# Linear attention with a gated FFN: loads of batch 2 no longer held for a weight, another buffer for batch 3's keys, an earlier wait for the weight load, a sketch by transposes, and a rebuilt order

## The chip, the cores and the metric

The kernel runs on one core of a Trainium2 chip. The metric is the device time of one execution in microseconds (us); lower is better. A profile also has a span, from the first to the last instruction of the profiled execution; it is some 2 us shorter than the time (97.4 against 95.4 in the profiled run of before). Runs are sorted by state: one over 1.5% above the fastest of its kernel counts as slow, and ratios use fast runs only. The engines are TensorE (PE in the views; PEld is its weight loads), VectorE (DVE), ScalarE (ACT), GpSimd (POOL) and SyncE (SP), which here issues loads and stores; a q behind a name means its sequencer.

## The reference

```python
# attention: batch 4, heads 4, seq 1088, head_dim 32, r = 8
phi(x) = outer(S1 x, S2 x).reshape(r * r)         # a polynomial sketch, 64 features
kv  = einsum('bhsf,bhsd->bhfd', phi(k), v);  z = sum_s phi(k)
out = einsum('bhsf,bhfd->bhsd', phi(q), kv) / (einsum(phi(q), z) + 1e-6)
# FFN on x = out, heads side by side (d_model 128, d_ff 1024)
x_prev = x shifted by one token
xk, xr = mu * x + (1 - mu) * x_prev               # with mu_k and mu_r
k = relu(xk @ w_k);  v = (k * k) @ w_v
result = sigmoid(xr @ w_r) * v
```

A batch's keys must all be summed into its state (kv, z) before its queries give x, and x opens its FFN.

## The kernel before

Each task has a name, an engine and a place in one long list; each engine does its tasks in the list's order. Those that matter here: KTb (DVE transposes the keys of batch b), KP and KA (projection, accumulation), QTb (DVE transposes the queries), Q1g (projection of the g-th of ten query groups), XK (the FFN's input, on DVE), M1 (first FFN product), Z (products of zeros that keep TensorE's clock up), DL3k, DL3v, DL3q (loads of batch 3). The other names in the cuts can be passed over.

```python
ORDER = """
SS/PE/b0 SM/DVE SC3/ACT SC1/POOL SC2/ACT SF/ACT KT0_0/DVE Z/4 S4T/PE/b0 S4E/ACT KT0_1/DVE Z/2 KP0_0/PE/b0 KE0_0/DVE
... (cut)
QX1/PE/b3 KT2_0/DVE KB1/ACT Q13/PE/b0 KT2_1/DVE XL0/ACT XP0/ACT XF0/POOL XB0/ACT KP2_0/PE/b1 QN2/DVE XP1/ACT DL3k/DMA
XK0/DVE QF2_1/POOL RR0/PE/b4 QE3/ACT XB1/ACT XK1/DVE M10_5/PE/b2 M10_3/PE/b5 SG0/ACT DL3v/DMA M10_2/PE/b6 KE2_0/ACT
... (cut)
"""
# input buffers: three sets for four batches
hdk.append(hdk[2]); hdq.append(hdq[1]); vt.append(vt[1])      # batch 3 shares
# SyncE's queue, in order: k0 v0 q0 k1 wr v1 q1; then, in the task WL,
def load_w():
    nc.gpsimd.tensor_copy(wk[:, :1], hdq[0][:, 0, :1])        # makes the weights wait for q0
    nc.gpsimd.dma_start(wk[:], moe_w_k)
    nc.gpsimd.dma_start(wv[:] ...)
    nc.sync.dma_start(turn[:], wk[:1, :1])                    # the "turn": SyncE waits for wk
    load_k(2, nc.sync); load_v(2, nc.sync); load_q(2, nc.sync)
add("DL3k", ..., load_k(3, nc.sync), ["KT2_0", "KT2_1"])      # k3 goes where k2 was
add("DL3v", ..., load_v(3, nc.sync), ["DL3k", "KA1_0_0", "KA1_1_0"])
add("DL3q", ..., load_q(3, nc.sync), ["DL3v", "QT1_0", "QT1_1"])
# the sketch: two products with an identity
nc.tensor.matmul(p[:, x * R:x * R + R], S8[:, x]..., ident[:R, :R], skip_group_check=True)
```

## Time and profile before

| | before |
|---|---|
| time, median (lowest to highest) | 97.13 us (96.3 to 97.21) |
| profiled span | 95.4 us |
| busy: PE, DVE, ACT, POOL | 81.9, 73.1, 64.4, 53.9 us |
| first FFN product; last product | 26.53; 88.11 us |

The prediction shows the busy slices, the chain of waits, the queue's waits and the stretches. One more view: busy time in two stretches, up to 40 us and from there on. Columns: stretch, length, then PE, PE's weight loads, DVE, ACT and POOL busy with instruction counts, granted clock, DMA share, GB/s.

```profile
0.00:40.00 40.00, 33.90 (x595) 24.62 (x595) 26.71 (x79) 19.49 (x62) 17.45 (x38) 1.00 0.70 184
40.00:96.00 56.00, 48.01 (x668) 35.38 (x668) 46.34 (x103) 44.95 (x84) 36.41 (x35) 0.96 0.18 42
```

DVE did 26.71 us of its work in the first 40 and left 46.34 us for the rest, during which it has hardly a hole.

### The profile page before, as it was taken

The page shows a single profiled execution, that of the slowest core. Times are in us where ns is not written, and L with a number is a line of the kernel's source. Part 1 is how long each engine was busy: PE and PEld are TensorE (multiplying, and loading weights), DVE is VectorE, ACT ScalarE, POOL GpSimd, SP SyncE. Part 2 cuts the span into 40 slices and gives each one's busy share as a digit, 9 for nine tenths or more (in the row PEclk, how much of TensorE's full clock was granted, in tenths as well). Part 3 has the DMA queues.
Part 4 walks back from the last instruction along what each step waited for, and adds up shares of the span by engine and source line. Part 5 has one row for each costly group of instructions (what it writes and reads, how often), then busy time and mean ns, then how long its engine had stood idle before and what let it go on. Part 6 is the DMA issues. An engine that isn't in the chain of part 4 may idle for free.

```text
span 95.4 us, 3142 instructions
## 1 busy us (share of the span) xinstructions
PE 81.9 (86%) x1263; PEld 60.0 (63%) x1263; DVE 73.1 (77%) x181; ACT 64.4 (68%) x146; POOL 53.9 (56%) x72
## 2 busy tenths in 40 slices
PE   5999989699589866899999999999999999999000
...
DVE  4062998983795449999998998999899999997200
ACT  0630144146399699199999979668999999999000
...
DMA  2899999248978910011000021051400000532620
...
DMA packets 8668, 9.71 MB, mean 102 GB/s; under 512 B 716, under 2 KB 7502, under 8 KB 8654
## 3 DMA queue, kind: packets, MB, share of 16 engines
...
q0 software_dynamic: 416, 0.52, 3.2%
...
q8 instruction: 10, 0.16, 0.7%
q14 instruction: 4, 0.03, 0.1%
...
## 4 chain that ended last, share of the span: by engine, by line
PE 40%; ACT 21%; DMA 15%; DVE 9%; issue 5%; POOL 2%; SPq 1%; ACTq 1%; DVEq 0%
ACT k L628 9%; PE ps_h L620 8%; DMA hdq<-in_q_dram 7%; ACT k L639 6%; PE ps_o L649 6%; DMA hdk<-in_k_dram 5%; PE ps_qtp L555 4%; PE wt L262 4%; PE ps_abw L510 4%; DMA S<-in_S_dram 3%; PE ps_kv L417 3%; PE ps_kab L386 3%; PE ps_x L576 2%; ACT r L667 2%; DVE kT L379 2%
## 5 line engine op out<-in xcount | busy, mean ns | idle before, releaser
L637 POOL TENSOR_TENSOR k<-k 128x1024 bf16<-128x1024 bf16 (+2 forms) x18 | 28.4, 1588 | 5.9 <-ACT k L628 3.6
L628 ACT ACTIVATE k<-ps_h 128x512 bf16<-128x512 f32 (+3 forms) x48 | 23.0, 541 | 1.4 <-PE ps_h L620 1.2
L620 PE MATMUL ps_h<-XK,wk 128*128 128x512 bf16 (+3 forms) x80 | 20.1, 350 | 0.4 <-DVE XK L589 0.3
L630 DVE TENSOR_SCALAR k<-ps_h 128x512 bf16<-128x512 f32 (+3 forms) x32 | 19.4, 639 | 0.6 <-PE ps_h L620 0.4
L639 ACT ACTIVATE k<-k 128x1024 bf16<-128x1024 bf16 (+3 forms) x19 | 18.5, 1010 | 1.6 <-DVE k L630 1.5
L649 PE MATMUL ps_o<-wv,k 128*128 128x128 bf16 x272 | 18.6, 219 | 0.1
L649 PEld LDWEIGHTS <-k 128*128 128x128 bf16 x272 | 16.2, 98 | 3.5 <-ACT k L639 0.9
L369 POOL TENSOR_TENSOR kp<-ab 128x512 f32<-128x512 f32 (+1 forms) x7 | 8.8, 1261 | 9.9 <-DVE ab L276 6.1
L369 POOL TENSOR_TENSOR qp<-an,wsb 128x512 f32<-128x512 f32 x8 | 8.5, 1072 | 6.2 <-PE ps_qtp L555 3.4
L620 PEld LDWEIGHTS <-wk 128*128 128x128 bf16 x80 | 7.6, 116 | 4.6 <-issue 1.9
L555 PE MATMUL ps_qtp<-ident,qp 128*128 128x128 f32 x68 | 9.7, 278 | 0.5 <-DVE qp L369 0.5
L386 PE MATMUL ps_kab<-SW,kT 128*64 128x64 f32 x144 | 7.0, 246 | 2.7 <-DVE kT L379 2.7
L386 PEld LDWEIGHTS ps_kab<-SW,kT 128*64 128x64 f32 x144 | 5.9, 156 | 4.9 <-ACT XB L274 2.4
L510 PE MATMUL ps_abw<-SW,qT 128*64 128x96 f32 (+1 forms) x120 | 8.3, 258 | 0.4 <-ACT SW L274 0.3
L555 PEld LDWEIGHTS ps_qtp<-ident,qp 128*128 128x128 f32 x68 | 7.5, 142 | 1.7 <-DVE qp L369 0.6
L379 DVE STREAM_TRANSPOSE kT<-hdk 128x256 f32<-128x256 f32 (+1 forms) x16 | 6.0, 428 | 3.0 <-DMA hdk<-in_k_dram 3.0
L510 PEld LDWEIGHTS ps_abw<-SW,qT 128*64 128x64 f32 (+1 forms) x120 | 6.5, 144 | 2.6 <-ACT kvS L274 1.0
L262 PE MATMUL wt<-zero 128*128 128x512 f32 (+2 forms) x10 | 6.8, 795 | 1.0 <-DVE one L161 1.0
L493 DVE STREAM_TRANSPOSE qT<-hdq 128x832 f32<-128x832 f32 (+1 forms) x8 | 5.6, 703 | 2.6 <-DMA hdq<-in_q_dram 2.6
L274 ACT COPY qpT<-ps_qtp 128x512 f32<-128x512 f32 (+1 forms) x13 | 6.6, 543 | 0.7 <-PE ps_qtp L555 0.6
L417 PE MATMUL ps_kv<-kp,vt 128*32 128x64 f32 x288 | 6.2, 223 | 0.9 <-issue 0.9
L667 ACT ACTIVATE r<-ps_r 128x512 f32<-128x512 f32 (+3 forms) x10 | 5.5, 550 | 2.1 <-PE ps_r L662 2.0
...
## 6 DMA issues: line engine op xcount, KB each, us to landing
...
```

Of the source, the lines that this page charges most:

```text
L262: nc.tensor.matmul(wt[:, :m * P], zero[:], _ap(zero[:], [[0, m], [1, P]]), skip_group_check=True)
L369: eng.tensor_mul(o.rearrange("p t h i j -> p (t h) i j"), _ap(a_, [[sa, y], [1, R], [0, R]]), _ap(b_, [[sb, y], [0, R], [1, R]]))
L386: nc.tensor.matmul(p[64 * c:64 * c + 64, (t - t0) * 64:(t - t0) * 64 + 64], kT[b][:, t, 64 * c:64 * c + 64], SW[:, 0, :H, :2, :], skip_gro ...
L417: nc.tensor.matmul(kv[32 * h:32 * h + 32, :64], vt[b][:, h, T, :], kp[:, t, h].rearrange("p i j -> p (i j)"), start=(T == 0), stop=(T == 8 ...
L510: nc.tensor.matmul(p[lo:hi, t * 96:t * 96 + 96], qT[:, s + lo:s + hi], SW[:, (s + lo) // S, g % 2:g % 2 + H].rearrange("p h x r -> p (h x ...
L555: nc.tensor.transpose(p[:, t * P:t * P + P], qp[g][:, t, 2 * pair:2 * pair + 2].rearrange("p h i j -> p (h i j)"), ident[:])
L620: nc.tensor.matmul(h[:, :n * P], wkc[:, c // 4, c % 4], XK[:, F0[g] * P:(F0[g] + n) * P])
L628: nc.scalar.activation(o, i, RELU)
L630: nc.vector.tensor_scalar(o, i, 0.0, None, op0=mybir.AluOpType.max)
L637: (nc.vector if eng == "DVE" else nc.gpsimd).tensor_mul(k2[:, :, :n * P], k1[:, :, :n * P], k1[:, :, :n * P])
L639: nc.scalar.activation(k2[:, :, :n * P], k1[:, :, :n * P], mybir.ActivationFunctionType.Square)
L649: nc.tensor.matmul(o[:, t * P:t * P + P], k2s[g, j][:, c, t * P:t * P + P], wv[:, w * j + c, :], start=(j == 0 and c == 0 and t == 0), sto ...
```

## The change

The intent: no hole in the queue of loads, batch 3's keys loaded earlier, a shorter front, and a list of tasks rebuilt around that.

```diff
-    hdk.append(hdk[2])
-    hdq.append(hdq[1])
-    vt.append(vt[1])
+    for x in (hdk, hdq, vt):
+        x.append(x[1])
...
     load_q(1, nc.sync)
+    load_k(2, nc.sync)
+    load_v(2, nc.sync)
+    load_q(2, nc.sync)
     def load_w():
-        nc.gpsimd.tensor_copy(wk[:, :1], hdq[0][:, 0, :1])
+        nc.gpsimd.tensor_copy(wk[:, :1], vt[0][:, 0, 0, :1])
         ... (wk and wv as before)
-        nc.sync.dma_start(turn[:], wk[:1, :1])
-        load_k(2, nc.sync)
-        load_v(2, nc.sync)
-        load_q(2, nc.sync)
-    add("WL", {"POOL": 1.6}, lambda e: load_w(), ["Lq0"])
+    add("WL", {"POOL": 1.6}, lambda e: load_w(), ["Lv0"])
-    add("DL3k", ..., ["KT2_0", "KT2_1"])
+    add("DL3k", ..., ["KT1_0", "KT1_1"])
-    nc.tensor.matmul(p[:, x * R:x * R + R], S8[:, x]..., ident[:R, :R], skip_group_check=True)
+    nc.tensor.transpose(p[:, x * R:x * R + R], S8[:, x]..., ident[:R, :R])
-    wsb: bufs=2      K2B: {2: 8, 4: 1}
+    wsb: bufs=3      K2B: {2: 7, 4: 1}
 ORDER (cut: the whole list is new, with other engines for some tasks)
-... SF/ACT KT0_0/DVE Z/4 S4T/PE/b0 ... Z/2 KP0_0 ... Z/4 KA0_0_0
+... SF/ACT SC2/POOL Z/2 S4T/PE/b0 KT0_0/DVE ... Z/2 KP0_0 ... Z/5 KA0_0_0
-... KT2_0 KB1 Q13 KT2_1 ... XK0 ... XK1 M10_5 ...
+... XK0 KG1 XK1 KW1 M10_1 M10_3 M10_0 KT2_1 ... KT2_0 ...
```

More of the change, by code (lines that the diff above doesn't have):

```diff
@@ L28 @@
 ORDER = """
-SS/PE/b0 SM/DVE SC3/ACT SC1/POOL SC2/ACT SF/ACT KT0_0/DVE Z/4 S4T/PE/b0 S4E/ACT KT0_1/DVE Z/2 KP0_0/PE/b0 KE0_0/DVE
-KP0_1/PE/b1 KF0_0_1/DVE KF0_0_0/POOL KE0_1/ACT KF0_1_0/DVE Z/4 KA0_0_0/PE/b0 KA0_0_1/PE KF0_1_1/DVE KA0_1_0/PE
-QT0_1/DVE WL/POOL KA0_1_1/PE MU/PE/b1 KC0/ACT KZ0/DVE QT0_0/DVE OM/ACT KD0/PE/b0 KG0/PE KW0/ACT KT1_0/DVE Q10/PE/b1
-KB0/ACT WRP/ACT KT1_1/DVE WRC/ACT KP1_0/PE/b0 Q11/PE/b2 QE0/DVE KE1_0/ACT QP0/DVE KP1_1/PE/b3 QD0/DVE KF1_0_1/POOL
-KF1_0_0/DVE QE1/ACT QI0/DVE KE1_1/ACT QP1/DVE QN0/DVE QD1/DVE KF1_1_1/DVE KF1_1_0/POOL KA1_0_0/PE/b0 QI1/DVE QF0_0/DVE
@@ L34 @@
-Q12/PE/b7 QN1/DVE QF1_0/DVE QR0_0/PE/b1 KA1_1_0/PE QE2/ACT QT1_0/DVE QV0_0/ACT QP2/DVE QT1_1/DVE QR1_0/PE/b2 KC1/ACT
-QR0_1/PE/b1 QR1_1/PE/b3 QV0_1/ACT KZ1/DVE QV1_1/ACT QD2/DVE KD1/PE/b0 QV1_0/DVE KG1/PE QI2/DVE KW1/DVE QY0/PE/b2
-QX1/PE/b3 KT2_0/DVE KB1/ACT Q13/PE/b0 KT2_1/DVE XL0/ACT XP0/ACT XF0/POOL XB0/ACT KP2_0/PE/b1 QN2/DVE XP1/ACT DL3k/DMA
-XK0/DVE QF2_1/POOL RR0/PE/b4 QE3/ACT XB1/ACT XK1/DVE M10_5/PE/b2 M10_3/PE/b5 SG0/ACT DL3v/DMA M10_2/PE/b6 KE2_0/ACT
-QP3/DVE RR1/PE/b3 RE0_2/DVE RE0_5/ACT M11_5/PE/b4 QF2_0/POOL QD3/DVE RE0_3/ACT M11_2/PE/b6 KF2_0_0/DVE SG1/ACT
@@ L39 @@
-M11_6/PE/b2 Q14/PE/b5 RE1_2/ACT DL3q/DMA RE1_5/ACT QI3/DVE KF2_0_1/DVE RE1_6/ACT M11_0/PE/b6 SQ0_1/POOL M11_3/PE/b3
-M10_4/PE/b4 QE4/ACT QR2_1/PE/b7 QN3/DVE RE0_4/ACT KT3_0/DVE RE1_0/ACT QR2_0/PE/b1 QF3_1/POOL RE1_3/ACT M11_7/PE/b6
-QV2_1/ACT M11_1/PE/b4 QF3_0/DVE M10_1/PE/b3 KP2_1/PE/b2 RE1_7/ACT RE0_1/DVE SQ1_1/POOL QV2_0/ACT M10_0/PE/b7 RE1_1/DVE
-M10_6/PE/b6 QR3_1/PE/b0 RE0_6/ACT QT3_1/DVE SQ1_0/ACT QR3_0/PE/b1 SQ1_3/POOL KA2_0_0/PE/b6 QV3_1/ACT QT3_0/DVE
-QV3_0/ACT M21_0/PE/b4 KT3_1/DVE M21_1/PE RE0_0/ACT M11_4/PE/b0 SQ0_2/ACT M10_7/PE/b1 QY2/PE/b3 SQ0_0/POOL QX3/PE/b7
@@ L44 @@
-KE2_1/ACT QT2_0/DVE RE0_7/ACT QP4/DVE RE1_4/ACT KF2_1_0/POOL KF2_1_1/DVE SQ1_2/ACT KP3_1/PE/b0 QD4/DVE XB2/ACT
-QT2_1/DVE M21_2/PE M20_0/PE/b1 XP2/ACT M20_1/PE M21_3/PE SQ0_3/POOL M20_2/PE KE3_1/DVE KA2_1_0/PE XL1/ACT XB3/ACT
-XK2/DVE XF1/POOL XP3/ACT M20_3/PE RR2/PE/b2 KF3_1_1/POOL KZ2/DVE FN1/DVE RR3/PE/b3 KC2/ACT FN0/DVE SG2/ACT OD1_0/DMA
-XK3/DVE M12_5/PE/b6 M12_4/PE/b1 XE0/POOL SG3/ACT OD1_1/DMA KD2/PE/b4 KF3_1_0/POOL QI4/DVE KG2/PE RE2_5/ACT OD0_0/DMA
-RE2_4/DVE M13_0/PE/b3 KW2/ACT M13_2/PE/b7 KB2/ACT QN4/DVE M13_5/PE/b6 SQ2_2/ACT RE3_0/DVE Q15/PE/b4 QF4_1/DVE
@@ L49 @@
-QF4_0/POOL M13_3/PE/b3 RE3_2/ACT M13_1/PE/b0 QE5/DVE Q16/PE/b1 RE3_3/ACT RE3_1/DVE RE3_5/ACT M13_4/PE/b7 SQ3_1/POOL
-QP5/DVE QR4_0/PE/b3 QE6/DVE SQ3_0/ACT QD5/DVE M13_7/PE/b6 QP6/DVE M13_6/PE/b0 QI5/DVE QR4_1/PE/b5 QV4_0/DVE RE3_7/ACT
-M23_0/PE/b2 RE3_4/ACT QN5/DVE QV4_1/DVE M12_6/PE/b3 RE3_6/ACT M12_7/PE/b6 QF5_1/POOL M12_3/PE/b7 QF5_0/DVE M23_1/PE
-SQ3_2/ACT KP3_0/PE/b5 QY4/PE/b0 RE2_7/DVE SQ3_3/POOL QR5_1/PE/b4 RE2_3/ACT RE2_6/DVE QR5_0/PE/b6 KE3_0/ACT QD6/DVE
-QV5_1/ACT M23_2/PE KF3_0_0/DVE QV5_0/ACT M12_0/PE/b3 QI6/DVE M12_2/PE/b4 M12_1/PE/b7 QN6/DVE RE2_0/ACT KF3_0_1/POOL
@@ L54 @@
-QX5/PE/b6 RE2_2/DVE RE2_1/ACT QF6_1/DVE SQ2_0/ACT SQ2_1/POOL M23_3/PE QF6_0/DVE KA3_0_0/PE/b5 FN3/DVE XL2/ACT XP4/ACT
-QR6_1/PE/b1 XP5/DVE XB4/ACT OD3_3/DMA KA3_1_0/PE QV6_1/ACT OD3_4/DMA XK4/DVE XF2/POOL RR4/PE/b2 XB5/ACT OD3_1/DMA
-XE1/POOL QR6_0/PE/b1 KZ3/DVE KC3/DVE OD3_2/DMA SG4/ACT XK5/DVE SQ2_3/POOL M14_0/PE/b5 OD3_0/DMA M14_1/PE/b0 QV6_0/ACT
-M14_5/PE/b7 RE4_0/DVE M14_3/PE/b2 KD3/PE/b6 RE4_3/ACT M14_2/PE/b1 RE4_1/DVE M14_4/PE/b5 KG3/PE RE4_2/ACT RE4_5/DVE
-M14_7/PE/b0 RE4_4/ACT M14_6/PE/b2 SQ4_1/POOL QY6/PE/b1 M15_7/PE/b4 RE4_7/DVE KW3/ACT M22_0/PE/b7 RE4_6/ACT RE5_7/DVE
@@ L59 @@
-Q17/PE/b5 KB3/ACT M22_1/PE QE7/DVE M22_2/PE QP7/DVE SQ4_2/POOL M22_3/PE QD7/DVE SQ4_0/ACT QI7/DVE Q19/PE/b4 QN7/DVE
-M15_3/PE/b6 FN2/DVE M15_2/PE/b2 SQ4_3/ACT M15_6/PE/b0 QF7_1/DVE M24_0/PE/b3 OD2_1/DMA M24_1/PE QF7_0/POOL RE5_2/DVE
-OD2_2/DMA RE5_3/ACT M24_2/PE OD2_3/DMA QE9/DVE SQ5_1/ACT M24_3/PE RE5_6/DVE OD2_0/DMA Q18/PE/b2 QP9/DVE FN4/DVE
-SQ5_3/ACT QR7_0/PE/b0 QD9/DVE QE8/DVE OD4_0/DMA QR7_1/PE/b3 QI9/DVE QV7_0/ACT QP8/DVE OD4_1/DMA RR5/PE/b5 QN9/DVE
-QD8/DVE QV7_1/ACT QF9_0/POOL OD4_2/DMA M15_0/PE/b0 QI8/DVE M15_5/PE/b6 QN8/DVE SG5/ACT OD4_3/DMA M15_4/PE/b7 QF8_0/DVE
@@ L64 @@
-QX7/PE/b3 RE5_0/ACT QF8_1/POOL RE5_4/DVE RE5_5/ACT QR9_1/PE/b0 QR9_0/PE/b7 XL3/DVE XP6/ACT SQ5_2/POOL XP7/DVE
-M15_1/PE/b6 QR8_1/PE/b2 XB6/ACT XK6/DVE QR8_0/PE/b4 XB7/ACT RR6/PE/b5 QV9_1/DVE RE5_1/ACT M16_0/PE/b1 QV8_0/DVE
-M16_4/PE/b0 SG6/ACT M16_6/PE/b6 XE2/POOL QV9_0/DVE RE6_4/ACT M16_1/PE/b4 XF3/POOL QV8_1/DVE M16_7/PE/b5 RE6_0/ACT
-SQ5_0/POOL RR7/PE/b0 RE6_1/DVE RE6_7/ACT M16_5/PE/b1 XK7/DVE RE6_6/ACT M16_3/PE/b2 M16_2/PE/b5 QY8/PE/b4 QX9/PE/b7
-SG7/ACT RE6_3/DVE SQ6_3/ACT SQ6_0/POOL RE6_5/DVE M17_1/PE/b2 M17_3/PE/b0 RE6_2/ACT XP8/DVE M17_2/PE/b3 M25_0/PE/b1
@@ L69 @@
-SQ6_2/ACT RE7_3/DVE M17_6/PE/b5 M25_1/PE RE7_6/DVE RE7_2/ACT M17_5/PE/b0 SQ6_1/POOL M17_7/PE/b6 XK8/DVE RE7_1/ACT
-M25_2/PE M26_0/PE/b3 RE7_5/ACT RE7_7/DVE M18_4/PE/b2 XB8/ACT M18_7/PE/b5 XP9/DVE M18_5/PE/b0 RE8_4/ACT M17_0/PE/b6
-RE8_7/DVE M18_3/PE/b4 SQ7_3/ACT XE3/POOL M25_3/PE RE8_3/DVE M26_1/PE SQ7_1/POOL FN5/DVE RE7_0/ACT M26_2/PE RE8_5/ACT
-M26_3/PE XK9/DVE OD5_1/DMA SQ7_0/ACT RR8/PE/b1 FN6/DVE OD5_2/DMA M18_1/PE/b0 M17_4/PE/b6 OD5_0/DMA M18_0/PE/b4
-RE8_1/ACT SQ8_2/POOL M18_2/PE/b3 RE7_4/DVE OD6_0/DMA M27_0/PE/b5 SG8/ACT OD6_1/DMA RE8_0/DVE M27_1/PE SQ7_2/ACT
@@ L74 @@
-OD6_3/DMA M18_6/PE/b1 RE8_2/DVE M19_1/PE/b6 OD6_2/DMA M19_5/PE/b4 M19_3/PE/b0 SQ8_0/ACT RE8_6/DVE M27_2/PE OD5_3/DMA
-M27_3/PE RE9_5/DVE SQ8_3/POOL SQ8_1/ACT M19_2/PE/b1 RE9_3/DVE M28_0/PE/b3 FN7/DVE M19_6/PE/b4 M19_0/PE/b0 RE9_1/ACT
-M28_1/PE RE9_6/DVE RE9_2/ACT OD7_2/DMA M28_2/PE RE9_0/ACT SQ9_1/DVE OD7_4/DMA M19_4/PE/b4 XB9/ACT M19_7/PE/b1
-SQ9_0/DVE OD7_1/DMA M28_3/PE RE9_4/ACT RE9_7/ACT OD7_3/DMA RR9/PE/b7 SQ9_2/DVE M29_0/PE/b4 OD7_0/DMA SQ9_3/ACT FN8/DVE
-M29_1/PE M29_2/PE SG9/ACT OD8_3/DMA M29_3/PE OD8_2/ACT OD8_1/DMA FN9/DVE OD8_0/ACT OD9_2/ACT OD9_0/ACT OD9_1/ACT
+SS/PE/b0 SM/DVE SC3/ACT SC1/POOL SF/ACT SC2/POOL Z/2 S4T/PE/b0 KT0_0/DVE S4E/ACT KT0_1/DVE Z/2 KP0_0/PE/b0 KE0_0/ACT
@@ new lines @@
+KP0_1/PE/b1 KF0_0_1/POOL KF0_0_0/DVE KE0_1/ACT KF0_1_0/DVE KF0_1_1/POOL Z/5 KA0_0_0/PE/b0 KA0_0_1/PE WL/POOL
+KA0_1_0/PE QT0_1/DVE KA0_1_1/PE MU/PE/b1 KC0/ACT KZ0/DVE QT0_0/DVE OM/ACT KD0/PE/b0 KG0/PE KW0/ACT KT1_0/DVE Q11/PE/b1
+WRP/POOL Q10/PE/b2 KB0/DVE KT1_1/DVE QE1/ACT WRC/POOL KP1_0/PE/b0 QE0/ACT QP1/DVE Q12/PE/b3 QP0/DVE QD1/DVE KE1_0/ACT
+QD0/DVE QI1/DVE QI0/DVE QN1/DVE KF1_0_0/POOL QN0/DVE QF1_0/DVE KP1_1/PE/b7 QE2/ACT KF1_0_1/DVE QR1_1/PE/b1 DL3k/DMA
+QF0_0/POOL KE1_1/ACT QR1_0/PE/b4 QP2/DVE KA1_0_0/PE/b0 QV1_1/DVE QV1_0/ACT KF1_1_1/DVE KF1_1_0/POOL QR0_0/PE/b2
@@ new lines @@
+QD2/DVE QR0_1/PE/b4 QI2/DVE QV0_0/DVE QV0_1/ACT QT1_0/DVE QY0/PE/b4 QX1/PE/b2 QT1_1/DVE KA1_1_0/PE XL0/ACT XP0/ACT
+XB0/DVE XF0/POOL XP1/ACT QN2/DVE KZ1/DVE DL3v/DMA KC1/ACT QF2_0/POOL XB1/ACT KD1/PE/b7 XK0/DVE KG1/PE XK1/DVE KW1/ACT
+M10_1/PE/b4 M10_3/PE/b0 M10_0/PE/b1 KT2_1/DVE Q13/PE/b5 KB1/ACT QF2_1/POOL RE0_1/ACT DL3q/DMA RE0_3/ACT RE0_0/ACT
+M11_2/PE/b4 KT2_0/DVE M11_4/PE/b0 M11_5/PE/b1 QE3/ACT M11_7/PE/b7 M11_6/PE/b2 RE1_4/ACT M11_0/PE/b6 SQ0_0/POOL QP3/DVE
+RE1_5/ACT M11_3/PE/b3 RE1_2/DVE M10_4/PE/b0 RE1_0/ACT KP2_0/PE/b1 SQ1_2/POOL QD3/DVE RE1_6/ACT RE1_3/DVE RE0_4/ACT
@@ new lines @@
+RE1_7/ACT M20_0/PE/b6 QI3/DVE M10_5/PE/b2 M10_2/PE/b4 M10_7/PE/b0 SQ1_1/ACT QR2_1/PE/b3 QN3/DVE RE0_2/DVE QF3_0/DVE
+QR2_0/PE/b7 RE0_7/ACT SQ0_1/POOL RE0_5/ACT QV2_1/ACT M11_1/PE/b0 QF3_1/DVE RR1/PE/b2 M10_6/PE/b4 RE1_1/ACT M20_1/PE
+SG1/ACT RR0/PE/b3 QT2_1/DVE KP2_1/PE/b0 SQ1_0/POOL SQ1_3/ACT RE0_6/ACT QR3_0/PE/b2 KE2_0/ACT QT2_0/DVE QV2_0/ACT
+QR3_1/PE/b4 SQ0_3/POOL KE2_1/DVE SQ0_2/ACT Q14/PE/b5 QV3_0/DVE KF2_0_1/POOL QV3_1/ACT KF2_1_1/DVE QY2/PE/b7 M20_2/PE
+SG0/ACT M20_3/PE QX3/PE/b4 FN0/DVE KF2_0_0/POOL KT3_0/DVE OD0_0/DMA M21_0/PE/b6 QE4/DVE M21_1/PE XP2/ACT XB3/DVE
@@ new lines @@
+KF2_1_0/POOL M21_2/PE KA2_0_0/PE/b1 XB2/ACT XK2/DVE M21_3/PE RR2/PE/b3 XP3/DVE M12_0/PE/b7 M12_1/PE/b2 SG2/ACT
+KA2_1_0/PE FN1/DVE XE0/POOL RE2_0/ACT KT3_1/DVE OD1_0/DMA M12_4/PE/b6 RE2_1/ACT M12_5/PE/b3 OD1_1/DMA M12_2/PE/b7
+KC2/DVE RE2_4/ACT KZ2/DVE M12_6/PE/b0 RE2_5/DVE KD2/PE/b1 SQ2_0/ACT KG2/PE RE2_6/DVE SQ2_2/POOL M12_7/PE/b3
+M12_3/PE/b6 KB2/DVE KP3_1/PE/b2 KW2/ACT QT3_1/DVE RE2_2/ACT Q15/PE/b1 RE2_3/ACT QP4/DVE RE2_7/ACT XL1/DVE Q16/PE/b6
+QT3_0/DVE SQ2_1/ACT XF1/POOL QD4/DVE M22_0/PE/b3 QI4/DVE QN4/DVE KP3_0/PE/b7 SQ2_3/ACT XK3/DVE QF4_0/POOL M22_1/PE
@@ new lines @@
+KE3_0/DVE M22_2/PE QE5/ACT QF4_1/DVE QE6/ACT KF3_0_1/POOL M22_3/PE KE3_1/ACT QP5/DVE M13_1/PE/b4 KF3_0_0/DVE
+M13_2/PE/b5 QR4_0/PE/b0 RE3_1/ACT KF3_1_0/POOL QD5/DVE FN2/DVE KA3_0_0/PE/b7 RE3_2/ACT QV4_0/ACT QI5/DVE M13_4/PE/b4
+OD2_3/DMA KF3_1_1/DVE M13_0/PE/b5 QR4_1/PE/b3 OD2_1/DMA RE3_0/ACT QN5/DVE M13_3/PE/b0 QP6/DVE OD2_2/DMA QF5_0/POOL
+QF5_1/DVE KA3_1_0/PE RE3_3/ACT OD2_0/DMA QV4_1/DVE M13_5/PE/b5 SQ3_1/ACT M13_7/PE/b0 SQ3_0/POOL M13_6/PE/b2 QD6/DVE
+QR5_0/PE/b3 KZ3/DVE RE3_4/DVE QR5_1/PE/b1 KC3/ACT RE3_6/ACT QI6/DVE KD3/PE/b7 QY4/PE/b4 QN6/DVE QV5_0/ACT KG3/PE
@@ new lines @@
+QV5_1/DVE KW3/ACT RR3/PE/b2 RE3_5/ACT KB3/DVE QF6_1/POOL QF6_0/DVE QX5/PE/b1 RE3_7/ACT SQ3_2/ACT SQ3_3/POOL Q17/PE/b0
+XP4/DVE XL2/ACT XB4/ACT QR6_1/PE/b6 XB5/DVE QE7/ACT RR4/PE/b5 SG3/ACT QP7/DVE Q18/PE/b7 XP5/ACT XK4/DVE XF2/POOL
+M23_0/PE/b2 QD7/DVE SG4/ACT QV6_1/DVE XE1/POOL M14_7/PE/b4 M14_1/PE/b3 QI7/DVE M14_5/PE/b5 RE4_7/DVE M14_4/PE/b6
+RE4_1/ACT M23_1/PE QN7/DVE RE4_4/ACT M14_0/PE/b4 RE4_5/DVE QF7_1/POOL M14_3/PE/b3 M23_2/PE RE4_0/ACT QF7_0/DVE
+M14_2/PE/b5 SQ4_2/ACT M14_6/PE/b6 RE4_3/DVE SQ4_0/POOL QR6_0/PE/b4 QR7_0/PE/b0 QE8/DVE RE4_2/ACT QV6_0/DVE QR7_1/PE/b3
```

37 lines of the change are left out of this document (28 added, 9 removed).

## The prediction

> **What bounds the kernel now.** I read four views of the trace before the change: the busy slices, the chain that ended last, the queue's own waits, and busy time by stretch. In the slices (40 of 2.385 us each; tenths busy):
>
> ```profile
> PE   5999989699589866899999999999999999999000
> DVE  4062998983795449999998998999899999997200
> ACT  0630144146399699199999979668999999999000
> DMA  2899999248978910011000021051400000532620
> ```
>
> Two regimes show. From slice 17 (about 40 us) to slice 36 all three compute engines stand at 8 to 9 tenths; before that they have holes, and the DMA row falls to 2 and 4 tenths in slices 7 and 8 (16.7 to 21.5 us) though seven of the twelve q, k, v loads are still to come. The chain names the hole; its columns are start, length, what:
>
> ```profile
> 18.71 0.56 SPq L233
> 19.27 0.05 issue
> 19.32 5.11 DMA hdk<-in_k_dram
> 24.43 0.03 issue
> 24.45 0.07 DVE kT L379
> ...
> 28.30 6.27 DMA hdq<-in_q_dram
> 34.57 0.02 issue
> 34.59 0.05 DVE qT L493
> ```
>
> L233 is the "turn": a one-element copy that makes SyncE hold the loads of batch 2 until the weight wk has landed. The queue's waits give its size, the engines' waits what is paid:
>
> ```profile
> SPq L233 <- DMA wk<-in_moe_w_k_dram: 11.6, 1, 11.6
> ...
> DVE kT L379 <- DMA hdk<-in_k_dram: 3.0, 2, 1.9
> DVE qT L493 <- DMA hdq<-in_q_dram: 2.6, 1, 2.6
> ```
>
> In numbers by stretch (us busy, instructions in brackets, clock, DMA share, GB/s):
>
> ```profile
> 15.00:20.00 5.00, 4.06 (x97) 3.34 (x97) 4.24 (x15) 1.37 (x5) 2.58 (x2) 1.00 0.52 91
> 20.00:25.00 5.00, 3.77 (x95) 2.61 (x86) 2.83 (x10) 3.15 (x12) 0.72 (x3) 1.00 0.83 236
> ...
> 35.00:40.00 5.00, 3.38 (x94) 2.95 (x94) 5.00 (x13) 2.94 (x8) 2.85 (x6) 1.00 0.00 0
> 40.00:50.00 10.00, 9.76 (x116) 7.33 (x117) 9.88 (x27) 9.45 (x20) 8.70 (x9) 1.00 0.07 21
> ```
>
> The columns after the length are PE, PE loads, DVE, ACT, POOL. Summed over the stretches from 40 to 88 us, PE is busy 47.7 of 48, DVE 45.9, ACT 44.8. So the back half is bound by the sum of work; the front half by loads and order. A change gains only by having **more work done before about 40 us**.
>
> **What the Trainium skill says.** "DMA: Bandwidth & Descriptors", section "Issuing engines are not separate DMA queues": transfers issued by SyncE, ScalarE and GpSimd run on the same 16 engines. The trace agrees: the DMA share is about 1.0 from 5 to 17 us whichever queue feeds it. The same page, "Queues, rings and completion order", says each DMA engine goes round-robin, by packet, between queues with work. The trace does not show that for the weights: they were issued at 10.92 and 11.68, but in the packet records counted by half microsecond the weight queue has none before 13.5, then 2, 17, 38, 56 while the SyncE queue falls 41, 34, 16, 5. The weights waited behind loads already queued. "TensorE: Matmul & The Clock Gate", Part 1, says the array runs at half clock until some 3.4 us of activity. This agrees: a 512-wide zero product took 2.08 us at 4.66, and 1.13 at 9.68. Its Part 4 has the transpose as a matmul in transpose mode against the identity; here the 128x128 f32 transpose (L312) is recorded as one pass, each f32 product of the sketch (L284) as two.
>
> **The change part by part.**
>
> (1) *The turn goes.* From the semaphores' records loads landed at: k0 4.5, v0 8.3, q0 9.4, k1 11.8, v1 15.0, q1 16.2, wk 18.4, wv 19.8, k2 24.4, v2 26.9, q2 28.0, k3 30.1, v3 33.5, q3 34.6. With the queue full, one 0.557 MB load follows another in about 2.15 us (k1 to v1 to q1; v2 to q2). The turn leaves about 3.4 us of empty queue (17 to 20.4), and the reload of batch 3, whose buffers come free late, some 1 us more near 26.5 to 28. In the changed kernel SyncE still waits before each load for the one eight places back, so k2 is issued at about 7, v2 by 9.5, q2 at 12. Batch 3 now reuses the buffers of batch 1 and waits for the k transposes of batch 1 (begun at 13.2 before) rather than those of batch 2. Estimate of landings: k2 18 to 19.5, v2 20 to 22.5, q2 24 to 25, k3 26.5, v3 28.7, q3 31. Each batch 2 load gains 3 to 5 us, q3 about 3.5. On the path that sets the end it is worth the 1.9 and 2.6 us DVE waits, and what PE loses with them.
>
> (2) *Weights wait for v0, not q0.* By itself this gains nothing: the cast that begins it ran at 10.42, behind a 1.07 us GpSimd product (9.41 to 10.48), not behind q0 (9.43). In the new order two such products precede it; with the faster front of (3) it starts near 10.3, as before. Its 3.0 us of transfer (14.5 to 17.5 in the trace) now stands among k2 and v2. I put wk at 19 to 22, wv at 21 to 24.
>
> (3) *Front: transposes and zeros.* The second half of the sketch ran 4.13 to 4.73 after its DMA; two single passes for four save about 0.25. The zero product after it shrinks from 512 columns (2.08 cold) to 256 (about 1.06), and the 128x128 transpose that waited behind it until 6.52 can go at 5.5. Sum: the first projection starts at about 6.7 instead of 7.7, roughly 1.1 us earlier. The copy after it moves to ACT, idle there. I carry 1.1 to 1.4 us to the first key state (12.7 before); k1, landing at 11.8, caps more.
>
> (4) *Order.* Before, the DVE sat at the k2 transposes until 24.45, and the XK product that opens the FFN, behind them in its queue, ran at 26.04; the first FFN product at 26.5. In the new order the x product stands ahead of the last key accumulation and XK ahead of the k2 transposes. Adding DVE durations from the first key state on (12.71 before): transposes and key copy 2.2, normaliser pieces of groups 0 and 1 1.4, features, evacuations and group 2 3.3, q1 transposes and rest 2.0: 8.9 us, so XK at 21.6, and 20.5 with (3). wk may bind: I take the **first FFN product at 21.5 to 22, 4.5 to 5 us earlier**.
>
> (5) *Totals.* Counting tasks that change engine: 33 go DVE to ACT and 37 ACT to DVE, small copies, near even; ten features go DVE to GpSimd and seven back (net 2 us off DVE); eleven ACT tasks go to GpSimd, eight squares come back (0.8 us off ACT). DVE plus ACT falls from 137.5 to about 134.5 us. Zeros and sketch take some 1.5 off PE.
>
> Now the end. *By DVE and ACT*: before, 26.4 of their 137.5 us were done at 26.5; the rest plus 12.7 idle, halved, gives the end near 88. After, about 22.0 done by 21.8 (k2 transposes and some evacuations come later, features have left), 111.8 to go, the same idle: 21.8 + 124.5/2 = 84.0, a gain of 4. *By PE*: before, 59.2 busy and 2.6 idle from 26.5 to 88.3. After, 2.2 us (Q13, first k2 projection, RR0) have slipped behind the FFN start: 21.8 + 61.4 + 2.6 = 85.8, a gain of 2.5. PE busy time is padded by waits inside matmul spans, so the truth lies between: 3.3. The tail of 7 us after the last product (88.4 to 95.4) keeps its form. 97.13 - 3.4 = **93.7 us**.
>
> **Rivals.** *Weights starve.* If the software queue is served only when SyncE's queue is dry, wk lands after q3, near 31 to 32, the FFN starts five us later than before, and the time is about 100. For it: the packet counts above. Against it: ScalarE's small mu loads, issued at 1.71 and 2.02, landed at 4.6 and 4.8 while SyncE's queue was full until 15, so a second queue is not locked out, only held behind what was fetched. A chance of one in twelve. *The back half takes it back.* PE, DVE and ACT already have 95% from 40 us on; if the new order leaves more bubbles there (bank and buffer reuse, squares on GpSimd at 1.90 us), half the gain goes: 95.5. For it: a hand-made order meets true durations for the first time. *The loads were hidden anyway.* The DMA waits on DVE sum to only 5.6 us and PE idles only 4.7 from 15 to 40; without the reordering the removal of the turn alone would give 1 to 2 us: 95.5 to 96. Against it: the order was rebuilt around the loads.
>
> **Range and chances.** Centre 93.7. The two sums span 2.5 to 4, and the bubble rival pulls one side, a denser front (up to 5) the other: 91.6 to 96.2. Faster by over 2% means below 95.19: that needs a gain of 1.95, below both sums, but the rivals stand near it: 0.77. Within 2%: 0.16; slower, the starving weights, 0.07.
>
> **What would show it.** The queue's waits without L233; the DMA row at 8 to 9 without a break to slice 12; k2's transposes and q3's with no DMA wait; first FFN product before 22.5; PE idle from 15 to 40 under 3.5 us; last PE product near 85. The prediction is wrong if PE waits on wk beyond 23, if the clock row or zero products show a cold array into the first projection, or if the DVE and ACT stretches after 40 fall under 9 tenths.

## The result, and the profile after

| | before | after |
|---|---|---|
| time, median | 97.1 us (four runs beside the changed kernel) | 92.95 us (92.07 to 95.15; the last is slow) |
| profiled span | 95.4 us | 90.0 us |
| busy: PE, DVE, ACT, POOL | 81.9, 73.1, 64.4, 53.9 | 78.2, 72.5, 62.0, 58.2 |
| first FFN product; last product | 26.53; 88.11 | 22.34; 83.79 |

The ratio is 0.956, 95% interval 0.9453 to 0.9666. A ratio is the mean time of one kernel's fast runs over that of the other's fast runs of the same rounds, so it is not quite the ratio of the medians. The kernel's output is correct.

The busy slices after (40 of 2.25 us each, counted from 0):

```profile
PE   5669999977799999999999999999999999989300
DVE  4051878998979889998998699999999999999200
ACT  0621223426879657997899879998999999999000
DMA  2899999999994010200112000002410002234420
```

The DMA row has no break up to slice 11, and DVE's holes before, 3 to 5 tenths in slices 9 and 12 to 14, are gone. The stretches that the prediction showed of before, and the two long ones:

```profile
15.00:20.00 5.00, 4.48 (x108) 3.59 (x103) 4.72 (x18) 2.04 (x6) 3.57 (x3) 1.00 1.13 247
20.00:25.00 5.00, 3.75 (x93) 2.79 (x82) 4.52 (x13) 3.27 (x14) 3.61 (x7) 1.00 1.06 310
...
35.00:40.00 5.00, 4.91 (x111) 3.62 (x102) 4.82 (x16) 4.65 (x10) 2.58 (x4) 1.00 0.11 29
```

```profile
0.00:40.00 40.00, 35.06 (x642) 26.19 (x645) 30.63 (x91) 21.34 (x63) 23.84 (x46) 1.00 0.71 190
40.00:96.00 56.00, 43.17 (x616) 32.84 (x620) 41.87 (x94) 40.66 (x75) 34.36 (x32) 0.96 0.16 38
```

DVE did 3.92 us more by 40 us, and has 4.47 us less left; the span fell by 5.3. The queue's waits have no turn, only waits for buffers and, of 1.4 us at most, for earlier loads; DVE waits for no DMA at all. These are the queue's two longest waits before loads (of v3 and k3), then DVE's three longest:

```profile
SPq L180 <- PE ps_kv L419: 6.0, 1, 6.0
...
SPq L173 <- DVE pw L521: 3.4, 1, 3.4
```

```profile
DVE SW L297 <- PE ps_ss L280: 3.3, 1, 3.3
DVE kp L365 <- ACT ab L270: 2.0, 1, 2.0
DVE osb L672 <- PE ps_o L645: 1.1, 2, 0.7
```

Where the chain before ran through two loads (k2's and q3's), here it runs through work (start, length, what), apart from one line of "issue", to which I return:

```profile
22.04 0.37 PE ps_kf L443 x4
22.41 0.29 PE ps_h L616 x3
22.70 0.94 PE ps_abw L506 x16
23.63 0.56 PE ps_h L616 x4
24.19 0.66 issue
24.85 0.57 PE ps_h L616 x4
```

### The profile page after: what moved, and what is told of

Its sections match the earlier page's. It is cut to its first block, busy times and chain, and to the rows that moved or that the text cites. A ratio compares the mean times of both kernels' runs of the same rounds, so it can differ in the third digit from the quotient of the medians.

```text
span 90.0 us, 3132 instructions
## 1 busy us (share of the span) xinstructions
PE 78.2 (87%) x1255; PEld 59.0 (66%) x1263; DVE 72.5 (81%) x184; ACT 62.0 (69%) x137; POOL 58.2 (65%) x78
## 4 chain that ended last, share of the span: by engine, by line
PE 60%; DVE 17%; DMA 7%; issue 4%; ACT 3%; ACTq 1%; SPq 1%; POOL 0%; POOLq 0%
PE ps_o L645 11%; PE ps_h L616 9%; DVE k L626 8%; PE ps_abw L506 8%; PE ps_qtp L551 7%; PE ps_kab L382 6%; PE ps_x L572 4%; PE ps_kv L413 4%; DMA S<-in_S_dram 4%; PE wt L258 4%; DMA out_dram<-osb 3%; DVE XK L585 3%; DVE osb L672 2%; PE ps_kf L443 2%; PE ps_r L657 2%
## 5 line engine op out<-in xcount | busy, mean ns | idle before, releaser
L624 ACT ACTIVATE k<-ps_h 128x512 bf16<-128x512 f32 (+3 forms) x51 | 24.4, 549 | 2.6 <-PE ps_h L616 2.4
L635 ACT ACTIVATE k<-k 128x1024 bf16<-128x1024 bf16 (+3 forms) x20 | 19.3, 1003 | 0.1
L616 PE MATMUL ps_h<-XK,wk 128*128 128x512 bf16 (+3 forms) x72 | 18.2, 346 | 1.3 <-issue 0.7
L626 DVE TENSOR_SCALAR k<-ps_h 128x512 bf16<-128x512 f32 (+3 forms) x29 | 17.1, 633 | 0.8 <-PE ps_h L616 0.4
L365 POOL TENSOR_TENSOR kp<-ab 128x512 f32<-128x512 f32 (+1 forms) x9 | 10.8, 1219 | 4.8 <-ACT ab L270 4.4
L365 POOL TENSOR_TENSOR qp<-an,wsb 128x512 f32<-128x512 f32 x9 | 9.6, 1071 | 3.7 <-DVE an L537 3.0
L585 DVE SCALAR_TENSOR_TENSOR XK<-ps_x,mu,PP 128x512 bf16<-128x512 f32 (+8 forms) x13 | 6.9, 549 | 0.5 <-ACT XB L270 0.5
L672 DVE TENSOR_TENSOR osb<-ps_o,r 128x512 f32<-128x512 f32 (+3 forms) x10 | 6.0, 603 | 1.1 <-PE ps_o L645 1.1
L365 DVE TENSOR_TENSOR kp<-ps_kab,ab 128x512 f32<-128x512 f32 (+1 forms) x7 | 5.0, 714 | 2.1 <-ACT ab L270 2.0
L382 PE MATMUL ps_kab<-SW,kT 128*64 128x64 f32 x144 | 6.2, 239 | 0.0
```

The costliest lines, as they stand in the source:

```text
L365: eng.tensor_mul(o.rearrange("p t h i j -> p (t h) i j"), _ap(a_, [[sa, y], [1, R], [0, R]]), _ap(b_, [[sb, y], [0, R], [1, R]]))
L382: nc.tensor.matmul(p[64 * c:64 * c + 64, (t - t0) * 64:(t - t0) * 64 + 64], kT[b][:, t, 64 * c:64 * c + 64], SW[:, 0, :H, :2, :], skip_gro ...
L585: nc.vector.scalar_tensor_tensor(XK[:, b * S + s:b * S + s + m], tiles[f"x_{g}"][:, c0:c0 + m], mu_k, PP[:, b * XW + s:b * XW + s + m], op ...
L616: nc.tensor.matmul(h[:, :n * P], wkc[:, c // 4, c % 4], XK[:, F0[g] * P:(F0[g] + n) * P])
L624: nc.scalar.activation(o, i, RELU)
L626: nc.vector.tensor_scalar(o, i, 0.0, None, op0=mybir.AluOpType.max)
```

## The experiments

Twelve kernels ran. Names that begin with b_ start from the kernel before, with a_ from the changed one. Four or six runs of each were timed.

### 1. The turn alone

Before, with the turn out (b_noturn), and after, with it put back (a_turn).

```diff
 b_noturn:
     load_q(1, nc.sync)
+    load_k(2, nc.sync); load_v(2, nc.sync); load_q(2, nc.sync)
-        nc.sync.dma_start(turn[:], wk[:1, :1])
-        load_k(2, nc.sync); load_v(2, nc.sync); load_q(2, nc.sync)
 a_turn: the reverse
```

> The kernel before, with only the turn taken out: the loads of batch 2 are queued right behind q of batch 1, the old order stays. Theory (loads and order are both needed): k of batch 2 lands near 18 to 20 instead of 24.4, the wait of 1.9 us of DVE for it goes, the first FFN product comes at about 24.5 to 25 (the k transposes still stand ahead of XK), gain 1 to 2 us: 95.1 to 96.1. Rival A (the loads alone are the whole gain): 92.5 to 93.5. Rival B (the loads were hidden, the order is everything): 96.5 to 97.1.

> The changed kernel with the turn put back: SyncE holds k, v, q of batch 2 until wk has landed. Theory: k of batch 2 lands near 24.5, the DVE stands at its transposes from 22.5 for some 2 us, q of batch 2 and all of batch 3 come 3.5 to 4 us later; the first FFN product stays near 22.3 (XK is ahead of the wait). Time 1.5 to 3 us over the changed kernel: 94.3 to 95.8. Rival B (the loads were hidden, the order is everything): within 0.7 us of the changed kernel, 92.3 to 93.5.

b_noturn: 95.86 us, ratio 0.9882 (0.9736 to 1.0028), unclear by the rule, near 1.2% in the middle. That is the theory's range. a_turn: 92.65 us, ratio 0.9507 (0.9419 to 0.9594): the turn, put back, costs nothing that shows, so here the theory missed and rival B's range held. In b_noturn k2 landed at 17.3 instead of 24.4, yet DVE still waits for loads:

```profile
DVE kT L376 <- DMA hdk<-in_k_dram: 2.0, 1, 2.0
DVE qT L490 <- DMA hdq<-in_q_dram: 1.9, 1, 1.9
```

Both waits are now for batch 3. Its keys go into batch 2's buffer, so their load can be issued only after KT2 (22.7); it lands at 29.5, and q3, last in the queue, at 33.25. The chain of b_noturn says the same:

```profile
25.32 1.01 SPq L181
26.38 6.87 DMA hdq<-in_q_dram
33.32 0.92 issue
```

So without the hole in the queue DVE still waits 3.9 of its 5.6 us for loads, and now it is the shared buffer that makes these late.

### 2. The FFN opened ahead of the k transposes of batch 2, in the old order

My reading after the result was the prediction's: the early first FFN product carries the gain. The edit moves KT2 behind XK1 in the old list, with the turn and without.

```diff
-... QX1 KT2_0 KB1 Q13 KT2_1 ... KP2_0 ... DL3k XK0 ... XK1 M10_5 ... M10_2
+... QX1 KB1 Q13 ... XK0 ... XK1 KT2_0 KT2_1 DL3k M10_5 ... M10_2 KP2_0
```

The first attempt (b_xkfirst, b_both) left DL3k ahead of KT2: k3 then overwrote k2, both gave wrong results, and KT2 waited for k3. Their times (102.1 and 94.93 us) test nothing.

> The kernel before, turn kept, but the XK products of groups 0 and 1 stand ahead of the k transposes of batch 2 on DVE, and the first projection of batch 2 stands behind the first three FFN products on PE. Theory (both needed): the first FFN product comes at about 24 to 24.5, but the batch 2 and 3 loads still come as late, so the q wait of 2.6 us stays or grows: gain 0.5 to 1.5 us, 95.6 to 96.6. Rival B (order is everything): 94.0 to 95.0. Rival A: no change, 97.

> Both edits on the kernel before: turn out, XK ahead of the k transposes. Theory: first FFN product at about 23.5 to 24, no DMA wait on DVE, two thirds of the gain of the whole change: 93.8 to 95.0. Rival C (the gain lies in the rest of the new order, the moves between engines): no more than 1 us, 96 or above.

The mended pair:

> The kernel before, turn kept, XK ahead of the k transposes of batch 2, mended: the load of k of batch 3 now stands behind those transposes again (in the first try it overwrote their buffer, which made a wrong result and a wait of its own). Theory (the first FFN product sets the end, and turn and order are two ways to free the same XK): the first FFN product comes at about 24 to 25, the end some 68 to 69 us after it, 95.0 to 96.3. Rival (loads set the end): unchanged, 96.5 to 97.2.

> Turn out and XK ahead of the k transposes, mended in the same way. If turn and order free the same XK, the two together give hardly more than one alone: first FFN product 0 to 0.5 us before that of b_xkfirst2 or b_noturn, 94.3 to 95.8. Rival (they add up): 93.0 to 94.0.

Both give correct results, miss all that was expected, and are slower than before: 98.08 us, ratio 1.0147 (1.0076 to 1.0217), and 98.0 us, 1.0132 (1.006 to 1.0204). The first FFN product did come earlier than before, at 25.41 and 24.58 against 26.53, but KT2 slipped to 26.16 and 25.32. With it slipped k3's load, and q3 landed at 35.5 and 35.2, so that DVE waited 1.9 and 2.5 us for q3. The chain of b_xkfirst2:

```profile
28.76 0.61 SPq L181
29.42 6.04 DMA hdq<-in_q_dram
35.53 0.92 issue
```

The mean clock of b_both2 (0.955 to 0.980) may be part of its loss, that of b_xkfirst2 (0.974 to 0.984) hardly. So an earlier first FFN product does not bring the gain by itself: here it was paid for with later k transposes and later loads of batch 3.

### 3. All the new loads in the old order, and the old loads in the new order

This pair splits the change in two. b_loads has the old order, engines and front; a_oldloads the new ones with turn, wait for q0 and shared k buffer.

```diff
 b_loads (on top of b_noturn):
-    hdk.append(hdk[2])
+    hdk.append(hdk[1])
-    add("DL3k", ..., ["KT2_0", "KT2_1"])        # and DL3k moved up behind KP1_1
+    add("DL3k", ..., ["KT1_0", "KT1_1"])
     weights wait for v0 as in the change
 a_oldloads (on top of a_turn): the reverse, DL3k, DL3v, DL3q behind KT2_0
```

> The order, engines and front of the kernel before, with every load as in the changed kernel: no turn, weights after v0, the keys of batch 3 in batch 1's buffer and issued after batch 1's transposes. Correct result. Theory Q (new): in every run of the old order the chain of waits passes through the q load of batch 3, which lands at 34.6 (before) and 33.3 (turn out) because k3's buffer comes free only after batch 2's transposes; the end follows 60.4 to 61.1 us later. Then q3 should land near 30 and its DVE wait (1.9 us with the turn out) vanish: span about 91.8, ratio to before 0.955 to 0.965. Theory K: the old order's end stands 70.9 us after batch 2's k transposes whatever q3 does: transposes near 22.7, span 93.6, ratio near 0.985. The prediction's step (4), only an earlier first FFN product counts: it stays near 24.8, span 93.7.

> The complement: the changed kernel's order, engines and front with the loads of the kernel before (turn, weights after q0, k3 in batch 2's buffer, issued after batch 2's transposes). Correct result. Theory Q says the gain is mostly the late loads: k3 lands near 30.5 and q3 near 35 again; DVE waits for them return, but the new order puts q3's transposes later (they were due near 33 to 35), so some 1 to 2 us come back: span 91.5 to 92.5, ratio 0.965 to 0.975. The prediction's step (4), order carries it: as with the turn alone, span 91.1, ratio 0.95 to 0.955. If the loads are all of it: span over 94, ratio 0.985 or more.

| run | time | ratio (95%) | first FFN product | q3 landed | DVE's waits for loads |
|---|---|---|---|---|---|
| b_loads | 92.88 | 0.959 (0.9504 to 0.9676) | 24.94 | 28.6 | none |
| a_oldloads | 92.28 | 0.9535 (0.9463 to 0.9607) | 23.14 | 34.5 | 1.3 us, for keys |
| after | 92.95 | 0.956 (0.9453 to 0.9666) | 22.34 | 30.2 | none |

Either half alone gives the whole gain, as far as these intervals tell, and the two together give no more. b_loads came in the range of the theory that loads carry the gain, a_oldloads in that of the theory that the order does: each half is enough, and neither is needed. b_loads does it with a first FFN product 2.6 us later than the changed kernel's. a_oldloads does it with loads as late as before (q3 at 34.5, against 34.6); its list asks for them later, so only this is left of the 5.6 us that DVE waited before:

```profile
DVE kT L378 <- DMA hdk<-in_k_dram: 1.3, 1, 1.3
```

What the fast kernels share is the busy time by 40 us (b_loads, then a_oldloads):

```profile
0.00:40.00 40.00, 36.60 (x643) 26.44 (x646) 31.25 (x91) 23.26 (x73) 21.12 (x42) 1.00 0.68 189
40.00:96.00 56.00, 43.29 (x619) 32.60 (x619) 41.92 (x91) 40.83 (x75) 32.66 (x30) 0.95 0.16 38
```

```profile
0.00:40.00 40.00, 34.51 (x623) 25.75 (x625) 29.53 (x88) 20.40 (x62) 23.15 (x43) 1.00 0.74 189
40.00:96.00 56.00, 44.11 (x632) 33.69 (x638) 42.77 (x98) 41.61 (x76) 35.05 (x35) 0.95 0.16 38
```

The same sum for every correct run (DVE time left at 40 us is from this view; the rest is the span, less 40, less that). The profiled runs of a_turn, a_sfirst_turn and b_q3late count as slow; by clock only b_q3late (0.968) and b_both2 (0.955) stand out, the others have 0.979 or more:

| run | DVE left at 40 | span | rest |
|---|---|---|---|
| b_xkfirst2 | 47.2 | 96.8 | 9.6 |
| b_both2 | 47.0 | 96.3 | 9.3 |
| before | 46.3 | 95.4 | 9.0 |
| b_q3late (below) | 45.9 | 95.1 | 9.2 |
| b_noturn | 45.0 | 93.7 | 8.7 |
| a_sfirst (below) | 43.0 | 91.1 | 8.1 |
| a_turn | 42.8 | 91.1 | 8.3 |
| a_oldloads | 42.8 | 91.0 | 8.2 |
| b_loads | 41.9 | 90.4 | 8.5 |
| after | 41.9 | 90.0 | 8.2 |
| a_oldfront (below) | 41.8 | 89.8 | 8.0 |
| a_sfirst_turn (below) | 41.6 | 89.8 | 8.2 |

The span follows the DVE work left over; the rest, DVE's small holes and the 6 to 8 us after the last product, moves by 1.6 us at most. This is book-keeping and not yet a cause, but it fits two very different ways to the same end, which neither the first FFN product nor any one landing does. Nor does it single out DVE: between before and after, what ACT has left at 40 us falls by 4.3 us and what PE has left by 4.8 (4.6 to a_oldfront, whose trace lacks no FFN product), much as DVE's 4.5.

### 4. Only q3's transposes moved, in the kernel before

```diff
-... QR3_1 RE0_6 QT3_1/DVE SQ1_0 QR3_0 ... QV3_1 QT3_0/DVE QV3_0 ... KT3_1 ... XK3/DVE M12_5
+... QR3_1 RE0_6 SQ1_0 QR3_0 ... QV3_1 QV3_0 ... KT3_1 ... XK3/DVE QT3_1/DVE QT3_0/DVE M12_5
```

> The kernel before with one thing moved: the two tasks of DVE that transpose the q of batch 3 (1.2 us in all, not read before the eighth group of queries) go from ahead of batch 3's second k transposes to behind the last XK of the first half. Loads, turn and all else as before. Correct result. Theory Q: DVE's 2.6 us wait for q3 vanishes, and what stood behind it (k transposes, x products, the next FFN states) comes up to 2.6 us earlier while the batch 2 wait (1.9 us, transposes at 24.4) stays: span 92.8 to 93.8, ratio 0.972 to 0.985. Theory K (the end stands 70.9 us after batch 2's k transposes) and the rival 'the waits were hidden anyway': no change, span 95 to 95.5, ratio 0.995 to 1.005.

96.48 us, ratio 0.9904 (0.9826 to 0.9982): between the two theories, less than I expected. The wait for q3 is gone from DVE's waits. In the profiled run (a slow one) the two XK behind it came 1.8 and 1.5 us earlier (37.60 and 39.16 against 39.36 and 40.64), but DVE now waited 1.6 us for a copy by ScalarE and 0.6 for an FFN product, and q3's transposes still had to be done behind the second XK: the reciprocal that follows in both runs started only 0.1 us earlier (41.26 against 41.38). The chain from 27.2 to 38.5 us is TensorE work, and TensorE's granted clock dropped, which shows in the clock row of the slices and in the stretch from 25 us (the third column from the right):

```profile
PEclk9999999999975999999999999999999999999995
```

```profile
25.00:30.00 5.00, 4.35 (x46) 3.12 (x47) 4.30 (x15) 2.52 (x9) 3.27 (x4) 0.75 0.55 176
```

The profile of before has no such dip. All six runs of b_q3late had a mean clock of 0.968 to 0.975, while before's in the same rounds ran from 0.946 to 0.990. So removing the q3 wait alone is worth about 1% (0.2 to 1.7); how much of the rest the clock took, and how much was TensorE work queued behind the late k2 anyway, stays open.

### 5. The front

a_oldfront is the changed kernel with the sketch by products and zeros of 4, 2, 4. a_sfirst has the second sketch load first in SyncE's queue, since that load landed at 4.09 us in the profile of before but at 4.6 to 6.0 in those of the other kernels that issue it from ScalarE.

```diff
 a_oldfront: nc.tensor.transpose(...) -> nc.tensor.matmul(..., skip_group_check=True); Z/2 -> Z/4, Z/5 -> Z/4
 a_sfirst:
-    nc.scalar.dma_start(S8[:, 1], ...)
+    nc.sync.dma_start(S8[:, 1], ...)           # ahead of load_k(0)
```

> The changed kernel with the old front: the sketch by two products, zero products 4, 2, 4. Theory: from the landing of the sketch load to the first projection it takes 3.36 us instead of 2.42, and this 0.94 goes through to the end: 0.7 to 1.0 us over the changed kernel, 93.3 to 93.9. Rival (k of batch 1 or the weights cap it): within 0.3, 92.4 to 92.9.

> The changed kernel with the second sketch load issued first on SyncE's queue, ahead of k of batch 0, instead of second on ACT's. Theory (the late sketch load, landed 5.2 us in the changed kernel and waited for 1.5 us by PE, starts the chain): it lands at 2.1 to 2.5, the first projection starts at 5.7 to 6.2 behind the k load, the first FFN product comes 1 to 1.5 us earlier, time 91.2 to 91.9. Rival (v of batch 0 and k of batch 1 take its place): first FFN product within 0.4, 92.2 to 92.8.

a_oldfront: 91.96 us, ratio 0.9549 (0.9487 to 0.9612), so the new front gives nothing that shows at the end (expected were 93.3 to 93.9). From the second sketch product to the first projection takes 3.36 us in every run with the old front and 2.42 in the changed kernel: 0.94 us saved, and lost in the arrival of the sketch and in what follows.

a_sfirst: 93.72 us where 91.2 to 91.9 was expected, ratio 0.9712 (0.9642 to 0.9782), above the changed kernel's 0.956 with intervals that hardly overlap, although its first FFN product stands 0.9 us earlier, at 21.43. TensorE stopped in the middle of that FFN (timeline: start, length, engine, line, operation, tile, shapes, count, idle before):

```profile
22.66 0.63 PE L616 MATMUL ps_h<-XK,wk 128*128 128x256 bf16 x4
26.03 0.30 PE L616 MATMUL ps_h<-XK,wk 128*128 128x256 bf16 x1 [2.74 <-issue]
```

"issue" means that no wait in the profile explains the 2.74 us. The packet records do: in every run they have a queue of the kind "instruction" with ten packets of 16,384 bytes, and TensorE's recorded instructions (2,548 in the changed kernel) make 255 to a packet. The Trainium skill, "Runtime: NRT & Kernel Launch", section "Instruction fetch mechanics", says that a sequencer fetches its program in blocks of 16 KiB, 256 instructions, through its own DMA queue. The traces agree. The stop is before TensorE's recorded instruction 705 (counted from 0), here, in the changed kernel (its 0.66 us of "issue") and in b_loads (0.73); in a_turn it is before instruction 961, which is 705 + 256. In each of these the stopped instruction runs 1.3 to 1.6 us after a packet has ended, which is what a wait for its own instructions looks like. Counting blocks back and forth from 705, each packet moves some time after TensorE enters the block before the one it brings:

| run | enters block (instruction, at) | next block's packet moves | queue of loads |
|---|---|---|---|
| after | 1217, at 37.84 | 37.94 | empty |
| after | 1729, at 50.43 | 50.58 | empty |
| after | 449, at 17.89 | 22.20 to 23.29 | full |
| a_sfirst | 449, at 17.02 | 23.35 to 24.70 | full |
| a_turn | 449, at 18.81 | 21.50 to 22.62 | hole from 17 to 19, then filling |
| a_turn | 705, at 24.84 | 30.93 to 32.19 | full |

With an empty queue the packet moves 0.1 us later in these rows (up to 0.7 in others of after), with loads queued 4 to 6 (3.0 in one more of after, for the block entered at 24.85, but only 1.1 in a_oldloads, for the block entered at 24.72). TensorE needs about 7 us for 256 instructions there (17.89 to 24.85), so with a faster front it can use up the instructions it has before the next ones arrive.

### 6. The sketch load first, with the turn back

```diff
 a_sfirst, plus
+        nc.sync.dma_start(turn[:], wk[:1, :1]) and the loads of batch 2 behind it
```

> The changed kernel with the second sketch load first on SyncE's queue and the turn put back. With the sketch load first alone the first FFN product came 0.9 us earlier (21.43) but PE then stood 2.7 us at one product with nothing but issue before it, while a 16 KB packet of the queue kind 'instruction' moved only at 23.35 to 24.70. Theory I: PE waits there for its own instructions, whose packets stand behind the loads in a full queue; the turn leaves a hole for them (in the run with the turn alone the packet moved at 21.5 and this product did not stall). Then the 2.7 us stall is gone or under 0.7, the first FFN product stands near 21.5 and the span near 89 (67 us plus a stall of 0 to 0.7 later), ratio 0.935 to 0.95. Rival: the stall belongs to the product's place in the order (a bank or weights not seen by the profile): it stays 2 us or more, span near 91, ratio 0.97.

The packet moved at 20.53 to 21.48, and TensorE's 2.74 us became 0.3:

```profile
PE ps_h L619 <- issue: 0.3, 1, 0.3
```

That is what theory I expected and the rival excluded: the stop follows the packet and not the place in the order. Why the packet is late is less clear. TensorE entered the block from 449 at 16.25, and the packet did not use the hole that the turn left (DMA share 0.09 from 17 to 18 us); that queued loads hold it up fits the table, but is not shown. The first FFN product came at 20.66, the earliest of all, and the span was 89.8 where 89 was expected. DVE again waits for keys, 2.3 us of it for k2, which landed at 23.23:

```profile
DVE kT L378 <- DMA hdk<-in_k_dram: 3.5, 3, 2.3
```

The six times are 91.76, 92.05, 91.95, 89.73, 92.8 and 90.65: median 91.85. The stated ratio, 0.9338 (0.9239 to 0.9437), rests on the two lowest, because the lowest makes slow runs of the other four; the median over that of before in the same rounds (96.87) is 0.948. Whether this kernel beats the changed one (0.956) is not shown.

## Why the prediction was right or wrong

The time, 92.95 us against 93.7, lay in the range, on the likelier side, and nearly all that was listed to watch came true. Two of the listed signs of being wrong came true too. From 40 to 50 us DVE and ACT fell under 9 tenths (8.75 and 8.85 of 10 us, against 9.88 and 9.45 before). And the array was still cold at the first projection: 18 of its 36 products took 314 ns or more where the last 16 took 222 (in before, 28 did). One step failed, the fourth, and as both sums of the end rest on it, that the time came out so close is in part luck.

- **Step (1), the loads: right.** Measured landings, with the estimate in brackets: k2 17.8 (18 to 19.5), v2 22.2 (20 to 22.5), q2 24.4 (24 to 25), k3 26.6 (26.5), v3 29.2 (28.7), q3 30.2 (31). DVE's 5.6 us of waits for loads went to nothing. What the step did not see is how little the turn does without the rest: b_noturn gains about 1.2%, and b_loads, with k3's new buffer and the weights' earlier wait on top, 4.1%. These two were not separated.
- **Step (2), the weights: right.** wk landed at 18.9 (19 to 22), wv at 22.7 (21 to 24), and no first product waits for them. Nothing tells what the earlier wait is worth alone.
- **Step (3), the front: mis-sized, and without effect.** "I carry 1.1 to 1.4 us to the first key state" became 0.4 us (12.31 against 12.71), and the first projection, put at 6.7 instead of 7.7, began at 7.66. The saving in instructions was 0.94 us, but the sketch load landed 1.1 us later in this profile than in that of before, and a_oldfront ends no later.
- **Step (4), the order: the size about right, the role wrong.** "First FFN product at 21.5 to 22, 4.5 to 5 us earlier": it was 22.34, 4.2 earlier. But both sums of the end start from that product, and it does not carry the end. It came 1.1 us earlier in b_xkfirst2 and the time rose by 1.5%; in b_loads it came only 1.6 us earlier, at 24.94, and the whole gain came. In its place the runs show the sum that the prediction stated in its first part and then left: how much work is done before 40 us. That the new order, with its engines, front and buffers, is enough for the gain is shown (a_oldloads); why it is, stays open.
- **Step (5), the totals: the sum right, its parts not.** DVE plus ACT fell to 134.5 us, as worked out, but DVE fell by 0.6 us instead of 2 and ACT by 2.4 instead of 0.8: that the sum came out is luck. PE fell by 3.7 instead of 1.5, but the trace of after lacks eight FFN products (72 of 80 on their line, 1.1 us less than in a_oldfront); zeros and sketch gave 1.3 (6.8 to 6.1 and 1.2 to 0.5).
- **The end.** The two sums gave gains of 4 and 2.5, and 3.3 was taken. The profiles give 5.3 (4.5 less DVE work left at 40 us, 0.9 less of holes and tail), the medians 4.2. The tail, which was to keep its 7 us, took 7.2 from the start of the last product to the end before and 6.2 after. Some figures are slips: 134.5 less 22.0 leaves 112.5, not 111.8 (an end at 84.4); the centre takes off 3.4 where 3.3 was derived; DVE's sum from 40 to 88 us is 45.8; six of the twelve q, k, v loads were still to come at 16.7 us, not seven; and v2 to q2 took 1.1 us, not 2.15.
- **The rivals.** "Weights starve" fell: from 16.5 us on the two queues moved about equal numbers of packets. "The back half takes it back" is at most a part of it: DVE stays at 8 or 9 tenths in nearly every slice (6 in slice 22) and did less from 40 to 50 us (the 8.75 above), yet the gain came. "The loads were hidden anyway" gave the turn alone 95.5 to 96 us, and b_noturn measured 95.86. But what spoke against it, that "the order was rebuilt around the loads", is not needed for the larger gain: with every load changed, the old order does as well.

What is not settled: the effect of the order without its moves between engines, of the third wsb buffer and the seventh k2 buffer; and why the two halves do not add. The table of experiment 3 only shows that with either one DVE has 41.9 to 42.8 us left at 40, close to what the two give together.

## What to carry to other kernels

When an in-order engine stands at a load, follow the load back to what kept it from being issued: here a shared buffer as well as the gap in the queue that the eye found first. Two cures for one loss need not add, as here, so test each alone before crediting the one with the better story. Read a mark such as "the first product of the next stage" as a symptom; ask which engines are full afterwards, and how much of their work is left when they fill up.

## What the Trainium skill lacked or had wrong

- "Runtime: NRT & Kernel Launch", "Instruction fetch mechanics", calls the cost of crossing a 16 KiB boundary "mostly hidden" and does not say what it can be while the kernel's own loads fill the DMA engines. Here the packet then moved up to 6.3 us after TensorE entered the block before it, against 0.1 to 0.7 us in an empty queue, and its lateness stopped TensorE for 0.7 us in the changed kernel and 2.7 us in a_sfirst. The same section gives PE 128 KiB, 2048 instructions, and in a tip two lines of 16 KiB: the traces fit the second: a packet one block ahead, ten in a span of 2,548 recorded instructions of the changed kernel.
- "DMA: Bandwidth & Descriptors", "Queues, rings and completion order", has the round-robin by packet, which the trace of after fits for the weights from 16.5 us on (per half microsecond 38, 35, 41, 49, 62, 61, 52 packets of SyncE's queue and 27, 35, 39, 47, 65, 58, 50 of the weights'). It lacks the time until a queue gets its first turn: the weights were issued at 11.83 and 12.59, and their first packet moved 4.7 us after the first of these.
- No page looked at has the spread of a small first load: the second sketch load, issued at 1.35 to 1.38 us from ScalarE, landed between 4.1 and 6.0 us in the profiles here, a spread of more than the 0.94 us that the new front saves.
